# Attention's work list with empty places and one more place per step, dispatch weights of two experts in one operation, six weight blocks fetched earlier

## The chip, the cores and the metric

One core of a Trainium2 chip runs the whole program. The metric is the device time of one execution in microseconds (us); the median of three executions of the kernel before is 598.34 us.

## The reference

Three layers follow each other. B = 4 batches, H = 8 heads, S = 576 rows, 64 columns per head, 32 memory slots.

```python
a = softmax(phi, over S);  k_m = a^T k;  v_m = a^T v           # per batch and head
attn = softmax(q k_m^T / 8);  x = attn v_m                      # [4*576, 512]
p = domain_probs / sum                                          # 4 experts, dense
x = sum_e p[:, e] * (relu(x @ w1[e]) @ w2[e])                   # 512 -> 1024 -> 512
logits = x @ phi2;  d = softmax(logits, over all 2304 rows)
slot = d^T x;  slot_out[e] = relu(slot[e] @ v1[e]) @ v2[e]      # 8 experts, 4 slots each
out = softmax(logits, over 32 slots) @ slot_out                 # [2304, 512], f32
```

Here v1 and v2 are the 8 experts' weights of the third layer (moe2_w1, moe2_w2).

## The kernel before

**Units and steps.** The second layer runs in five units: units 0, 1 and 2 are batches 0, 1 and 2 with 576 rows, units 3 and 4 are the halves (288 rows) of batch 3. A unit has 8 steps, one for each half of an expert's 1024 columns. Units 3 and 4 do steps 0 and 1 together; then unit 3 does its steps 2 to 7, and then unit 4 (`MIX` is 2). A step consists of 8 places (4 for a unit of 288 rows alone). A place `at` begins with one `up`: six matmuls (lines 434 to 436) of the weights `G` with the attention result `A`, in high and low parts; ScalarE takes the result out of PSUM (line 444), and after every second `up` VectorE transposes it into `h` (line 446).

**What is put between the `up`s.** Place `at_g` (place 2 of a step with 8) issues `g_mult` for the next step: 16 matmuls (line 391) of the values `vb` with a block `raw` of w1, which SyncE fetched two steps before. Its two halves come out of PSUM in `g_out` at places 3 and 4, ScalarE (line 401) and VectorE (line 402). At place 0 the matmuls for the logits of the step before are issued (line 461). In the other places `pump` takes one entry from the list `fg` and one from the list `bg`, unless the `fg` entry is one of the heavy ones, which stand alone. An entry may be `None`: an empty place.

**The two lists.** `fg` holds the rest of the unit before: the logits' statistics, the weights `we` (line 601), five heavy blocks of `sums` (line 625, matmuls of `we` with `h`, accumulated into `srun` by VectorE, line 633 or 635), and the row softmax. `bg` holds the attention of the next batch, `attention(b)`: loads of phi, k and v; the softmax over S with the column maximum in two halves (line 159, `mx`), its turn through TensorE (lines 168, 172), the sums in two halves (line 207, `sm`) and a small matmul that gathers them (lines 243, 247); then five tiles of q, each with a turn (299), scores (315), exponential (330), normalisation (335 to 338) and a turn into `A` (346, 351, 352). Each engine runs its own instructions in the order in which the program issues them.

**Buffers.** PSUM has 4 rotating banks `at` for everything but `up` and the logits. SBUF has 2 buffers `raw`, 2 buffers `g` and 5 buffers `big`; k and v of the next batch take a `big` one, which comes free only when the `sums` of the unit before have read `h`. SyncE issues every DMA, in program order; where one waits for its buffer, all later ones wait behind it.

**The last stretch.** The third layer reads its weights in 160 blocks `v` of 256 KB each: 32 blocks of w2 (line 690), 64 of v1 (line 693) and 64 of v2 (lines 700 and 707). `fill` takes a buffer that has come free and fetches the next blocks of the list into it; `done` refills it once its blocks are used. Five blocks go early into buffers of attention, nine and then 36 into `big`, four into `A1`; after the `sums` of unit 4 come eight into `raw`, eight into `g` and four into `A0`. At the start of unit 4's step 2 the program stands thus:

```python
if us == (NU - 1,) and n == MIX:
    for _ in range(4):
        fill(bigp, "big", 9)
```

Blocks are used in the order in which they are fetched (lines 1000, 1026 and 1166).

**Unit 0** does more: in its steps 0 to 7 it also prepares `M` = w2 times phi2 (lines 488 to 514), in its step 0 it ends its own attention, and `shares` (four matmuls, line 821, and 20 copies, lines 826 and 830) spreads the shares `p`, which the `fg` entries of the unit read.

Of the kernel before, what the change touches and what calls it, by code (L numbers as in the profile page):

```python
# [8 lines left out]
F32 = mybir.dt.float32  # L9
F32R = mybir.dt.float32r  # L10
ACTF = mybir.ActivationFunctionType
ALU = mybir.AluOpType
# [4 lines left out]
def kernel(  # L17
# [23 lines left out]
    nc = tc.nc  # L41
# [3 lines left out]
    NSLOT = phi2.shape[1]  # L45
    FH = 512
    NCH = E * F // FH
# [34 lines left out]
    A = [const.tile([128, 2, 2, S], F32R, tag=f"A{n}", name=f"A{n}") for n in range(2)]  # L82
    kbd = [const.tile([128, 4, 2, NM], F32, name=f"kbd{n}") for n in range(2)]
    vb = [const.tile([128, 128], F32, name=f"vb{n}") for n in range(2)]
    M = const.tile([128, 4 * NCH, NSLOT], F32)
    srun = const.tile([128, 8, 4, 32], F32)
    mrun = const.tile([128, 1], F32)
    zrun = const.tile([128, 1], F32)
# [5 lines left out]
    def load_phi(b):  # L94

        t = att.tile([128, 36, NM], F32, tag="ph", name="ph")
        src = phi[b].rearrange("(i c) s m -> c i s m", c=2)
        for c in range(2):
            nc.sync.dma_start(
                out=t[:, 16 * c:16 * c + 16, :].rearrange("p (i r) m -> p i (r m)", i=4),  # L100
                in_=src[c, :, 0:512, :].rearrange("i (p r) m -> p i (r m)", r=4),
            )
        for c in range(2):
            nc.sync.dma_start(
                out=t[64 * c:64 * c + 64, 32:36, :],
                in_=src[c, :, 512:576, :].rearrange("i p m -> p i m"),
            )
        ph_t[b] = t
# [18 lines left out]
    def load_q(b, ti):  # L127

        t = att.tile([128, H, HD], F32, tag="q", bufs=2, name="q")
        if ti < 4:  # L130
            nc.sync.dma_start(
                out=t, in_=q[b, :, 0:512, :].rearrange("h (p r) d -> r p h d", r=4)[ti]
            )
        else:
            nc.sync.dma_start(out=t[0:64], in_=q[b, :, 512:576, :].rearrange("h s d -> s h d"))
        q_t[b, ti] = [t[:, 2 * j:2 * j + 2].rearrange("p c d -> p (c d)") for j in range(4)]
# [386 lines left out]
    def group(u):  # L523
# [10 lines left out]
        def share(e):  # L534
            return pe[:, b, tb0:tb0 + nt, e:e + 1].to_broadcast([128, nt, 32])
# [57 lines left out]
        def weights(h):  # L593

            def f():
                if h == 0:
                    st["dt"] = pc.tile([128, nt, 32], F32, tag="lt", name="dt")
                    nc.vector.transpose(out=flat(st["dt"]), in_=flat(st["lc"]))
                we = st["we", h] = pc.tile([128, nt, 2, 32], F32, tag="we", bufs=2, name="we")
                for e in range(2):  # L600
                    nc.vector.tensor_tensor(
                        out=we[:, :, e], in0=st["dt"], in1=share(2 * h + e), op=ALU.mult
                    )
                if h == 1:
                    nc.vector.tensor_copy(out=mrun, in_=st["mg"])
                    if st["first"]:
                        nc.vector.tensor_copy(out=zrun, in_=st["zg"])
                    else:
                        nc.vector.scalar_tensor_tensor(
                            out=zrun, in0=zrun, scalar=st["fo"], in1=st["zg"],  # L610
                            op0=ALU.mult, op1=ALU.add,
                        )
            return f
# [125 lines left out]
    with tc.manual_schedule():  # L739
# [94 lines left out]

        fg, bg, heavy = [], [], []

        def pump():


            f = fg.pop(0) if fg else None  # L840
            if f:
                f()
            if f in heavy:
                return
            f = bg.pop(0) if bg else None
            if f:
                f()

        def attention(b):

            kvs = kv_stages(b)
            qs = [q_stages(b, ti) for ti in range(5)]

            def load(*a):
                def f():
                    for g in a:
                        g()
                return f

            def with_q(f, m):  # L860
                def g():
                    f()
                    if m < 5:
                        load_q(b, m)
                return g
            items = [lambda: (load_phi(b), load_kv(b, 0)), lambda: load_kv(b, 1), kvs[0], kvs[1]]
            items += [kvs[2], None, kvs[3], lambda: load_q(b, 0), kvs[4]]
            items += [lambda: (load_q(b, 1), kvs[6]()), kvs[5], kvs[8], kvs[7], kvs[9], kvs[11], kvs[10]]
            items += [with_q(qs[0][0], 2), kvs[12], None, kvs[13]]
            for t in range(5):  # L870
                items.append(qs[t][1])
                items.append(with_q(qs[t + 1][0], t + 3) if t < 4 else None)
                items.append(qs[t][2])
                items.append(lambda t=t: (qs[t][3](), qs[t - 1][4]() if t else None))
            items += [None, qs[4][4]]
            return items
# [8 lines left out]
        def finish(lu, n):  # L885

            _, g_, sums, rows = groups[lu]
            if lu < NU - 2:
                rw = [None] * 5 + [f for row in rows for f in (row, None, None)]
            else:  # L890
                rw = [f for row in rows for f in (row, None)]
            if lu < NU - 2:
                ps_ = [sums(k, 5) for k in range(5)] if lu < NU - 3 else [sums(k, 4) for k in range(4)]
                fg.extend([None] * 3 + g_[:2] + [None] + g_[2:5] + [None] * 2 + ps_ + rw)
            else:
                ps_ = [sums(k, 2) for k in range(2)]
                fg.extend([None] + g_[:5] + ps_ + [None] * 4 + rw)
            heavy[:] = [g_[0]] + ps_
            if lu < NU - 3:
                bg.extend([None] * 8 + attention(lu + 2))  # L900

        for n, us in steps:
            b = units[us[0]][0]
            s = b * NCH + n
            ups = [
                (u, fb, ki) for fb in range(4) for u in us for ki in range(len(units[u][1]))
            ]
            if us == (0,) and n == 0:
                ups.sort(key=lambda x: x[2])

            if len(ups) == 8:
                at_l, at_g, at_c = 0, 2, (3, 4)
            elif n == MIX:
                at_l, at_g, at_c = 1, 2, (3,)
            else:
                at_l, at_g, at_c = int(us != (NU - 1,) or n > MIX), 0, (1, 2)
            if us == (0,) and n == 0:
                bg += attention(1)
                bg.insert(8, shares)
            if n == 0 and us[0]:  # L920
                assert len(bg) == 0
            if n % 2 == 0:
                for u in us:
                    hid_tile(u, n // 2)
            if us == (NU - 2,) and n == MIX:
                fill(att, "ph", 2, again=False)
                fill(att, "kt", 1, again=False)
                for _ in range(2):
                    fill(att, "q", 1, again=False, bufs=2)
            if us == (NU - 2,) and n == NCH - 1:  # L930
                fill(bigp, "big", 9)
            if us == (NU - 1,) and n == MIX:
                for _ in range(4):
                    fill(bigp, "big", 9)
            gs = []
            for at, (u, fb, ki) in enumerate(ups):
                up(u, n, fb, ki)
                if at in at_c and gs:
                    gs.pop(0)()
                if at == at_l:  # L940
                    for lu, ln in last:
                        logits(lu, ln)
                        if ln % 2:
                            groups[lu][0](ln // 2)
                        if ln == NCH - 1:
                            finish(lu, n)
                if at == at_g and s + 1 < NG and us != (NU - 1,):
                    gs = g_mult(s + 1)
                else:
                    pump()  # L950
                if us == (0,):
                    for f in early[at] if n == 0 else ():
                        f()
                    if n and at in (1, 2, 3, 4, 6, 7):
                        ms[n][(1, 2, 3, 4, 6, 7).index(at) + 1]()
                    if at == 5 and n + 1 < NCH:
                        ms[n + 1][0]()
            for f in gs:
                f()
            last = [(u, n) for u in us]  # L960
        (lu, ln), = last
        logits(lu, ln)
        groups[lu][0](ln // 2)
        fill(const, "A1", 4, again=False)

        g_ = groups[lu][1]
        warm2(8)
# [5 lines left out]
        warm2(6)  # L973
        for _ in range(2):
            fill(rawp, "raw", 4)
        for _ in range(2):
            fill(gp, "g", 4)
        fill(const, "A0", 4, again=False)
        rest = groups[lu][3]

# [240 lines left out]
```

## Time and profile before

| What | Value |
|---|---|
| Median of three executions | 598.34 us (596.36 to 599.28) |
| The profiled execution: time, span | 600.98 us, 599.1 us |
| TensorE matmul busy | 551.8 us, 92% |
| VectorE, ScalarE busy | 313.4 us (52%), 204.2 us (34%) |
| Mean granted TensorE clock | 0.981 of full speed |
| HBM read, written | 100.50 MB, 4.72 MB |

The span is the time from the first to the last instruction; 1.9 us of the profiled execution lie around it. TensorE's share is the union of its matmuls, of which up to a few overlap, so 92% does not say that the array works at its peak; what can be gained is read from what TensorE waits for, stretch by stretch. Unit 1 runs from about 165 to 277 us of the span, unit 2 from 277 to 388, and the last stretch, from the end of unit 4's sums, from 504 on. In the rows, "PE" is TensorE, "PEld" its weight loads, "DVE" VectorE, "ACT" ScalarE, "SPq" the issuing of DMAs by SyncE, and L159 is line 159 of the kernel.

### The profile page before, as it was taken

Reading aid. Unit: us, or ns where it says so; the run is one execution under the profiler, and the core shown is the slowest. Engines: PE = TensorE matmul, PEld = TensorE weight load, DVE = VectorE, ACT = ScalarE, POOL = GpSimd, SP = SyncE. Lnnn points to the kernel's source line nnn. Section 1 sums busy time; section 2 is a strip of 40 time slices with the busy share of each in tenths; the row PEclk is TensorE's granted clock in tenths of the full one; section 3 lists DMA queues with packets and bytes.
Section 4 is the critical chain, followed back from the end, with each engine's and each line's share of the span. In section 5 each row is a group of like instructions: output and inputs, shape, how many; then the busy total and the mean of one; then the engine's idle time right before and its main releaser. Section 6 shows DMA issues by size and latency. Waiting matters only on the chain.

```text
span 599.1 us, 15721 instructions
## 1 busy us (share of the span) xinstructions
PE 551.8 (92%) x6810; PEld 390.6 (65%) x6810; DVE 313.4 (52%) x693; ACT 204.2 (34%) x509; POOL 28.3 (5%) x34
## 2 busy tenths in 40 slices
PE   8887999999999899999989999999989998999993
PEld 7675778777776668877657787766557685324342
DVE  5656646864581566677345677761567362012022
ACT  2332445444451244554123344530444130102022
POOL 0000000101000001100000101000010000000000
PEclk9989999999999889999998899999999999999998
DMA  8992455444141733332446232440550398999998
GB/s 216 317 317 72 159 160 167 142 141 142 71 148 46 234 94 102 102 124 71 121 132 197 81 105 72 130 170 4 174 196 0 120 369 300 361 355 388 360 352 279
DMA packets 92771, 106.22 MB, mean 177 GB/s; under 512 B 30752, under 2 KB 55840, under 8 KB 92704
## 3 DMA queue, kind: packets, MB, share of 16 engines
q1 hardware_dynamic: 92704, 105.24, 54.2%
q8 instruction: 53, 0.87, 0.6%
q14 instruction: 14, 0.11, 0.1%
HBM read 100.50 MB, written 4.72 MB: 176 GB/s over the span
## 4 chain that ended last, share of the span: by engine, by line
PE 65%; DVE 14%; DMA 11%; issue 4%; ACT 3%; SPq 1%; POOL 0%; ACTq 0%; DVEq 0%; POOLq 0%
PE mm L434 11%; DMA v<-in_moe_w_dram 11%; PE at L625 9%; PE mm L436 9%; PE mm L435 9%; PE lb L461 6%; PE at L391 5%; DVE g L402 3%; PE at L315 3%; DVE h L446 2%; PE at L488 2%; PE mm L767 2%; PE at L299 1%; PE at L223 1%; ACT hT L444 1%
## 5 line engine op out<-in xcount | busy, mean ns | idle before, releaser
L444 ACT ACTIVATE hT<-mm 128x288 f32<-128x288 f32 x256 | 105.1, 411 | 235.0 <-PE mm L436 204.2
L446 DVE STREAM_TRANSPOSE h<-hT 128x576 f32<-128x576 f32 (+1 forms) x160 | 104.0, 652 | 138.6 <-ACT hT L444 126.8
L434 PE MATMUL mm<-A,g 128*128 128x288 f32 x512 | 170.4, 333 | 2.1 <-ACT g L401 1.0
L436 PE MATMUL mm<-A,g 128*128 128x288 f32 x512 | 153.2, 299 | 2.6 <-DVE g L402 2.6
L435 PE MATMUL mm<-A,g 128*128 128x288 f32 x512 | 152.6, 298 | 0.8 <-DVE A L352 0.8
L434 PEld LDWEIGHTS mm<-A,g 128*128 128x128 f32 x512 | 98.0, 191 | 48.9 <-ACT hT L444 20.4
L436 PEld LDWEIGHTS mm<-A,g 128*128 128x128 f32 x512 | 97.8, 191 | 3.9 <-DVE g L402 3.9
L435 PEld LDWEIGHTS mm<-A,g 128*128 128x128 f32 x512 | 98.3, 192 | 1.3 <-DVE A L352 1.0
L625 PE MATMUL at<-h,we 32*32 32x256 f32 x2304 | 58.3, 385 | 6.3 <-issue 4.4
L625 PEld LDWEIGHTS at<-h,we 32*32 32x32 f32 x2304 | 34.7, 103 | 25.5 <-issue 10.7
L402 DVE TENSOR_TENSOR g<-at,g 128x512 fp32r<-128x512 f32 x64 | 42.5, 671 | 5.5 <-ACT g L401 5.3
L461 PE MATMUL lb<-hT,M 128*32 128x288 f32 x512 | 40.8, 425 | 1.6 <-DVE M L514 1.6
L401 ACT CAST g<-at 128x512 fp32r<-128x512 f32 x64 | 37.2, 583 | 0.0
L391 PE MATMUL at<-raw,vb 64*32 64x512 f32 x512 | 36.5, 601 | 0.3 <-DVE srun L635 0.2
L1166 PE MATMUL mm<-v,hz 128*8 128x256 f32 x256 | 34.4, 380 | 0.6 <-DVE mm L1053 0.6
L1166 PEld LDWEIGHTS mm<-v,hz 128*8 128x8 f32 x256 | 13.3, 88 | 19.9 <-DMA v<-in_moe_w_dram 5.2
L488 PE MATMUL at<-ident,w 128*128 128x128 f32 x128 | 20.5, 284 | 3.3 <-issue 1.3
L461 PEld LDWEIGHTS lb<-hT,M 128*32 128x32 f32 x512 | 13.1, 111 | 15.0 <-issue 5.8
L541 DVE STREAM_TRANSPOSE lt<-lb 128x288 f32<-128x288 f32 x32 | 14.6, 470 | 14.6 <-PE lb L461 13.7
L1026 PE MATMUL mm<-v,sT 128*32 128x512 f32 x128 | 21.2, 597 | 0.9 <-DMA v<-in_moe_w_dram 0.5
L488 PEld LDWEIGHTS at<-ident,w 128*128 128x128 f32 x128 | 14.6, 143 | 10.6 <-issue 3.1
L552 POOL TENSOR_TENSOR lt<-lt,pe 128x576 f32<-128x576 f32 (+1 forms) x10 | 9.9, 989 | 226.3 <-DVE lt L541 226.3
(153 smaller groups left out, 523.7 us busy)
## 6 DMA issues: line engine op xcount, KB each, us to landing
v<-in_moe_w_dram SPq DMA_DIRECT2D x160, 256.0 KB, 5.7
raw<-in_moe_w_dram SPq DMA_DIRECT2D x32, 1024.0 KB, 5.1
w<-in_moe_w_dram SPq DMA_DIRECT2D x16, 512.0 KB, 6.9
kv<-in_k_dram SPq DMA_DIRECT2D x8, 512.0 KB, 4.8
kv<-in_v_dram SPq DMA_DIRECT2D x8, 512.0 KB, 6.1
out_dram<-ot SPq DMA_DIRECT2D x16, 256.0 KB, 4.1
q<-in_q_dram SPq DMA_DIRECT2D x12, 256.0 KB, 5.3
ph<-in_phi_dram SPq DMA_DIRECT2D x8, 256.0 KB, 5.6
```

Source lines behind the costliest of these rows:

```text
L391: nc.tensor.matmul(ts[c][32 * i:32 * i + 32, :], vb[b % 2][64 * c:64 * c + 64, 32 * i:32 * i + 32], raw[s][64 * c:64 * c + 64, i, :], star ...
L401: nc.scalar.copy(out=hi, in_=t)
L402: nc.vector.tensor_tensor(out=lo, in0=t, in1=hi.bitcast(F32), op=ALU.subtract)
L434: nc.tensor.matmul(ps, gh, ah, start=(c == 0), stop=False)
L435: nc.tensor.matmul(ps, gh, al, start=False, stop=False)
L436: nc.tensor.matmul(ps, gl, ah, start=False, stop=(c == 1))
L444: nc.scalar.activation(out=t[:, o0 - base:o1 - base], in_=ps, func=ACTF.Relu)
L446: nc.vector.transpose(out=hid[u, n // 2][:, :, 4 * (n % 2) + fb], in_=t[:, 0:o1 - base])
L461: nc.tensor.matmul(lb[u, ki][32 * a:32 * a + 32, 0:o1 - o0], M[:, 4 * n + a, :], hT[u, n, a][:, o0 - base:o1 - base], start=(f == 0), stop ...
L488: nc.tensor.transpose(t[:, 128 * c:128 * c + 128], st["w"][:, a, 128 * c:128 * c + 128], ident)
L625: nc.tensor.matmul(ts[p][32 * e:32 * e + 32, 0:256], st["we", e // 2][rows, tb, e % 2], hid[u, e][rows, tb].rearrange("p k f -> p (k f)"), ...
L1166: nc.tensor.matmul(accs[acc][32 * i:32 * i + 8, 0:256], hz[:, dh != 2, f, i, :], blk[:, 256 * m:256 * m + 256], start=(dh == 2 and f == 0) ...
```

## The change

There are five edits.

1. `pump` gets a flag. At the place of `g_mult` it now runs for `bg` alone, so that `bg` has 8 places per step and `fg` still 7.
2. Attention's list has empty places again (`lead` of them after the loads, and single ones), its loads stand three entries earlier, and a few entries change order: the sums' second half directly before the second heavy matmul block, the turn of k before the first half of v.
3. In unit 0 both halves of `g_out` run at place 3, and `shares` stands at place 3 of step 0, in one of the empty places.
4. `weights` makes `we` of two experts in one multiplication with four-dimensional operands, in place of two.
5. `fill(gp, "g", 4)` stands at the start of unit 4's step 2, in front of the four fills of `big`, in place of one of the two after the sums; `M`'s buffer, free after the last logits, takes two blocks after `A1`'s.

```diff
+    M = const.tile([128, 4 * NCH, NSLOT], F32, tag="M", name="M")
...
-                for e in range(2):
-                    nc.vector.tensor_tensor(
-                        out=we[:, :, e], in0=st["dt"], in1=share(2 * h + e), op=ALU.mult
-                    )
+                nc.vector.tensor_tensor(
+                    out=we, in0=st["dt"].unsqueeze(2).to_broadcast([128, nt, 2, 32]),
+                    in1=pe[:, b, tb0:tb0 + nt, 2 * h:2 * h + 2].unsqueeze(3).to_broadcast(
+                        [128, nt, 2, 32]
+                    ), op=ALU.mult,
+                )
...
-        def pump():
+        def pump(both=True):
...
-            f = fg.pop(0) if fg else None
+            f = fg.pop(0) if fg and both else None
...
-            items = [lambda: (load_phi(b), load_kv(b, 0)), lambda: load_kv(b, 1), kvs[0], kvs[1]]
-            items += [kvs[2], None, kvs[3], lambda: load_q(b, 0), kvs[4]]
-            items += [lambda: (load_q(b, 1), kvs[6]()), kvs[5], kvs[8], kvs[7], kvs[9], kvs[11], kvs[10]]
-            items += [with_q(qs[0][0], 2), kvs[12], None, kvs[13]]
+            items = [lambda: (load_phi(b), load_kv(b, 0)), lambda: load_kv(b, 1)] + [None] * lead
+            items += [kvs[0], kvs[1], kvs[2], None, None, kvs[3], lambda: load_q(b, 0), kvs[4], kvs[5]]
+            items += [lambda: (load_q(b, 1), kvs[6]()), kvs[7], kvs[8], kvs[9], None, kvs[10]]
+            items += [kvs[11], with_q(qs[0][0], 2), kvs[12], None, kvs[13]]
...
-                bg.extend([None] * 8 + attention(lu + 2))
+                bg.extend([None] * 5 + attention(lu + 2, 5))
...
-                bg += attention(1)
-                bg.insert(8, shares)
+                bg += attention(1, 4)
+                bg[3] = shares
...
             if us == (NU - 1,) and n == MIX:
+                fill(gp, "g", 4)
                 for _ in range(4):
...
                     gs.pop(0)()
+                    if us == (0,):
+                        gs.pop(0)()
...
-                else:
-                    pump()
+                pump(not gs or at != at_g)
...
         fill(const, "A1", 4, again=False)
+        fill(const, "M", 2, again=False)
...
-        for _ in range(2):
-            fill(gp, "g", 4)
+        fill(gp, "g", 4)
```

## Rows read from the trace of the kernel before

**Rows 1.** The page: busy share of the DMA engines in 40 slices of 15 us.

```profile
DMA  8992455444141733332446232440550398999998
```

**Rows 2.** The chain that ended last, stretch from 490 us (start, length, what).

```profile
507.89 6.60 DMA v<-in_moe_w_dram
...
574.15 4.02 DMA v<-in_moe_w_dram
```

**Rows 3.** Windows of the last stretch: busy time, then clock, DMA share, GB/s.

```profile
490.00:500.00 10.00, 9.44 (x245) 7.41 (x243) 3.93 (x12) 1.21 (x4) 0.00 (x0) 1.00 1.05 382
500.00:510.00 10.00, 7.58 (x127) 4.41 (x131) 2.58 (x7) 0.59 (x1) 0.52 (x1) 1.00 0.75 247
```

**Rows 4.** Waits of SyncE's queue: us in total, times, longest.

```profile
SPq L122 <- PE at L625: 35.5, 2, 18.4
SPq L690 <- PE at L625: 34.6, 1, 34.6
...
SPq L693 <- PE at L625: 3.7, 1, 3.7
```

**Rows 5.** Waits from 507 to 586 us.

```profile
PEld mm L1026 <- DMA v<-in_moe_w_dram: 9.5, 19, 1.4
```

**Rows 6.** TensorE's timeline at the end of unit 4's step 2.

```profile
456.22 0.29 PE L436 MATMUL mm<-A,g 128*128 128x288 f32 x1
```

**Rows 7.** Waits of TensorE in unit 1 (165 to 277 us).

```profile
PE at L172 <- DVE mx L159: 2.3, 2, 1.2
PE at L346 <- DVE ex L338: 1.0, 1, 1.0
PE at L243 <- DVE sm L207: 0.9, 1, 0.9
```

**Rows 8.** Windows in unit 1: busy time, then clock, DMA share, GB/s.

```profile
200.60:204.00 3.40, 1.66 (x12) 1.21 (x10) 3.29 (x5) 1.67 (x5) 0.00 (x0) 1.00 1.02 280
204.00:207.40 3.40, 2.83 (x12) 2.83 (x13) 1.94 (x4) 0.41 (x1) 0.00 (x0) 0.50 1.06 362
...
221.07:224.48 3.41, 3.41 (x24) 2.29 (x28) 1.07 (x5) 0.41 (x1) 0.00 (x0) 0.50 0.02 5
```

**Rows 9.** The chain from 196 to 222 us, unit 1 (start, length, what).

```profile
195.99 0.70 PE at L625 x31
...
202.07 0.93 DVE mx L159
...
203.59 0.94 DVE mx L159
...
205.04 0.24 PE mm L434
...
208.09 0.14 PE mm L434
...
211.78 1.02 PE at L391 x16
...
219.70 0.93 DVE sm L207
```

**Rows 10.** VectorE's timeline there; in brackets its idle time before.

```profile
200.71 0.78 DVE L446 STREAM_TRANSPOSE h<-hT 128x576 f32<-128x576 f32 x1 [1.95 <-ACT hT L444]
```

**Rows 11.** SyncE's timeline in unit 1.

```profile
196.51 1.74 SPq L122 DMA_DIRECT2D kv<-in_k_dram  x2
...
200.86 1.35 SPq L370 DMA_DIRECT2D raw<-in_moe_w_dram  x1
```

**Rows 12.** That block of `raw` alone: us from issue to landing.

```profile
DMA to landing us min/median/max: 9.1/9.1/9.1
```

**Rows 13.** TensorE's timeline in unit 0, steps 0 and 1.

```profile
47.54 0.33 PE L172 MATMUL at<-ident,mx 128*128 128x128 f32 x1 [1.80 <-DVE mx L159]
...
57.43 0.63 PE L488 MATMUL at<-ident,w 128*128 128x128 f32 x4 [1.35 <-issue]
```

**Rows 14.** Instructions that read or write `pe`: ns min, median, max; starts; forms.

```profile
L601 DVE TENSOR_TENSOR we<-dt,pe x20: 417/718/759, 173.2 to 495.4; 128x576 f32<-128x576 f32 x12, 128x288 f32<-128x288 f32 x8
L826 DVE COPY pe<-at x16: 135/158/159, 56.9 to 58.3; 128x16 f32<-128x16 f32 x16
...
L830 DVE COPY pe<-at x4: 149/150/150, 57.2 to 58.4; 128x8 f32<-128x8 f32 x4
```

More of the change, by code (lines that the diff above doesn't have):

```diff
@@ L84 @@
     vb = [const.tile([128, 128], F32, name=f"vb{n}") for n in range(2)]
-    M = const.tile([128, 4 * NCH, NSLOT], F32)
+    M = const.tile([128, 4 * NCH, NSLOT], F32, tag="M", name="M")
     srun = const.tile([128, 8, 4, 32], F32)
@@ L847, in pump, with attention @@
                 f()
-        def attention(b):
+        def attention(b, lead):
             kvs = kv_stages(b)
```

## The prediction

> **What bounds the kernel now.** I read the page first, then the chain that ended last, then each stretch's waits. The page's DMA row splits the run: after the first three slices mostly 1 to 5 tenths, 0 in slice 30 (from 450 us), then 8 or 9 in every slice from 480 us on [rows 1]. The chain agrees: from 507.89 us it runs from one transfer of `v` to the next, to 578 us [rows 2]. So the last stretch ends when the last `v` block has come; TensorE waits there for blocks with time to spare, 9.5 us in the v1 phase alone [rows 5]. Before that TensorE is the bound, and what can be won is its idle time. In unit 1 three waits make 4.2 us of it, all on VectorE, for `mx`, for `ex` and for `sm` [rows 7]; the same three, equally long, stand in unit 2. Behind two of them the granted clock is 0.50 for 3.4 us, that is 1.2 of 2.4 GHz, and matmuls come every 0.24 us instead of 0.14 [rows 8, 9].
>
> **Edit 5, the six blocks.** SyncE's order decides. The second fill of `big` waits 34.6 us for the `sums` of unit 3 [rows 4], and meanwhile nothing moves [rows 1]. The four `g` blocks are now in front of it. Their buffer is that of unit 4's step 2, whose last matmul is at 456.22 us [rows 6]; they are issued just behind that and land in the idle time before 472 us. The only thing queued behind them on SyncE is the fill of `big` that waits anyway. At 382 GB/s a block of 262,144 bytes takes 0.69 us [rows 3], so four taken out of the full stretch are worth 2.7 us. Nothing excludes less, if the stream stops later for a buffer: bound 0.
>
> The two `M` blocks go into a hole. SyncE has no buffer left and waits 3.7 us for unit 4's `sums` [rows 4]; the rate falls from 382 to 247 GB/s over 10 us, which is 1.35 MB or 3.5 us lost [rows 3]. Two more blocks fill 1.4 us of it for certain. If the queue does not run empty, its slow restart goes too, and all 3.5 us come back. I take 2.2 us, nearer to the sure part, because the two blocks alone cover less than half of the wait. One of the two later `g` fills remains; its buffer (unit 4's `h`) is released by the same `sums`. Should it get the buffer of the four early blocks instead, it would wait for the w2 phase to read them, some 3 us after the last `raw` issue, with eight transfers under way to cover it: at most 1 us. Edit 5: -4.9 us, between 0 and -6.2.
>
> Beside the row stands a page: the Trainium skill, "DMA: Bandwidth & Descriptors", section Specifications, gives about 358 GB/s from HBM to one core. The trace's 382 GB/s over 10 us is above it [rows 3]. By the page a block would take 0.73 us and edit 5 would give some 0.2 us more.
>
> **Edits 1 and 2 in units 1 and 2.** I wrote down for both kernels which entry falls on which place. Three things move.
>
> `mx`: before, its halves are issued at places 3 and 4 of step 2 and the turn at place 5, and VectorE does `g_out` and `mx` in turn, 0.93 us each time for `mx` [rows 9], while TensorE stands 2.3 us. After, the first half is issued at place 2, where VectorE is idle for 1.95 us [rows 10], the second at 3, the turn at 4. VectorE saves one `mx` and one `g_out` of the queue, TensorE arrives one `up` (0.8 us) earlier. That leaves 2.3 + 0.8 - 0.93 less part of a 0.65 us `g_out`, some 1.8 us: -0.5.
>
> `sm`: the second half moves from place 6 to place 4, the matmul that needs it from 7 to 6. VectorE has done it when TensorE comes: of 0.9 us [rows 7] I leave 0.1: -0.8.
>
> `ex`: the last normalisation now has `g_mult` (1.02 us [rows 9]) between it and its turn. Of 1.0 us [rows 7] I leave 0.1: -0.9.
>
> Half speed: about 14 matmuls at 0.24 instead of 0.14 us [rows 9] make some 1.4 us for each of the two spells in a unit. The one behind `sm` should go with its wait, the one behind `mx` may stay, as 1.8 us of standing remain. I take one of two: -1.4.
>
> What it costs: k and v are now asked for in step 0, and SyncE waits there for the `big` buffer until the `sums` end, as before [rows 4]. Now the `raw` block of step 1 is queued behind it. Before, the block issued in that spot (for a step later) went at 200.86 us and landed 9.1 us later [rows 11, 12], 13.3 us after the `sums` end at 196.7; `g_mult` comes 15.1 us after it [rows 9], and with the savings above about 12.9. So a wait of 0.4 us, 0.2 on average over the two clock cases. And five more entries per unit now stand behind `g_mult`, which holds two of the four banks: no row shows the price; between nothing (VectorE and ScalarE are idle there, [rows 10]) and one `g_out` (0.65 us) each, 3.3 us. I take 0.8.
>
> Per unit -0.5 - 0.8 - 0.9 - 1.4 + 0.2 + 0.8 = -2.6, for both -5.2. Bounds: 0 (each stall only moves) and, with all waits and half-speed spells gone, 2 x (4.2 + 2.8) = -14.
>
> **Edits 1 to 3 in unit 0.** The wait for `mx` (1.80 us) and the one behind `shares` (1.35 us) [rows 13] go, since `mx` gets two places more and `shares` leaves step 1. In step 0 `shares` puts 20 copies of 0.15 us [rows 14], overlapped some 1.6 us, ahead of VectorE's share of unit 0's last q tiles, for which the next `up` waits: +1.2 to +1.6, less what that wait hides. -3.15 + 1.6 = -1.5; bounds 0 and -3.1.
>
> **Edit 4.** 288 more elements cost 0.30 us (718 against 417 ns) [rows 14], so 1152 cost 0.72 + 0.60 = 1.32 against 1.44 us: 0.1 us for each of ten. Only in unit 4, where nothing else runs, are two of them on the path: -0.2. Above, if the four-dimensional form cost as much more as 288 further elements, 0.3 us each: +0.6.
>
> The Trainium skill, "VectorE: DVE Perf Modes", section on the TRN2 errata, says that a VectorE operation between SBUF tensors pays a fixed 58 cycles (60 ns) each. By that the ten would save 0.6 us in all, by the rows 1.2; on the path 0.1 against 0.2.
>
> **The sum.** -4.9 - 5.2 - 1.5 - 0.2 = -11.8 us. The profiled execution took 600.98 us, so 589.2; it lies 2.6 us over the median of 598.34, which becomes 586.5. A change under 0.5% (3 us) cannot be told from none here.
>
> **The rivals.**
> - *Only the last stretch gains* (0.20). VectorE has the same work in a unit; a wait taken from `mx` or `sm` may come back at an entry behind `g_mult`. For it: VectorE is 3.29 of 3.40 us busy around the `mx` wait [rows 8]. Against: right before that it is idle 1.95 us [rows 10]. 598.3 - 4.9 - 0.2 = 593.2.
> - *Only the front gains* (0.08): the stream is held up again by a buffer, so that 160 blocks end no earlier. Against: TensorE's 9.5 us of waiting [rows 5]. 598.3 - 6.9 = 591.4.
> - *More than forecast* (0.07): no half-speed spell is left and the hole in the stream closes wholly: 2.8 + 1.3 + 1.6 us more, 580.8.
> - *Nothing to be measured* (0.08): half of the last stretch, the rest given back: 596.
> - *Slower* (0.07): the `raw` block that now waits behind k and v. Every us by which it comes after `g_mult` stands in full, once in unit 1 and once in unit 2. To eat 11.8 us and 3 more it has to be 7.4 us late each time, 20 us after the `sums` end instead of 13.3. For it: 9.1 us to land [rows 12] while k and v are moving at 362 GB/s [rows 8]. Against: it is now the first block behind them, as the later one was. From 7.4 us on it decides; at 8 us the time is 602.5.
>
> **The numbers.** My forecast has 0.50: 586.5, own range 581 to 591. The range of 8 in 10 takes in the gain in the last stretch alone and the larger gain: 578 to 594. Faster by over 0.5%: 0.50 + 0.20 + 0.08 + 0.07 = 0.85; within: 0.08; slower: 0.07.
>
> **What would show it.** In the changed kernel's trace: four `v` blocks issued near 450 us and the DMA share no longer falling between 502 and 507 us; the last `v` earlier by 5 us relative to unit 4's `sums`; in units 1 and 2 the `sm` and `ex` waits gone, `mx` still there at under 2 us, two clock falls instead of four; `shares` at some 39 us; ten `we` operations of 1.3 and 0.7 us. It is wrong if TensorE's idle time in units 1 and 2 stays at 4 us each, if `g_mult` waits for a DMA in step 3, or if the `v` stream shows a new gap.

## The result and the profile after

The changed kernel takes 580.88 us (median of four executions, 580.06 to 581.87), the kernel before 598.81 us (four, 596.36 to 601.11): ratio 0.9702, interval 0.966 to 0.9744. The forecast was 586.5 us with a range of 578 to 594. The profiled execution took 581.87 us, its span is 579.9 us, that is 19.1 us less than before.

Where the 19.1 us are is read from two points in each trace. Unit 4's `sums` end at 490.2 us instead of 504.0: 13.8 us come from the units ahead of it. From there to the end of the span it is 89.7 us instead of 95.1: 5.3 us come from the last stretch. Of the 13.8 us, 12.1 are in units 1 and 2, which run from 159.8 to 379.4 us in before and take 207.5 us after instead of 219.6; a unit is counted here from ScalarE's last copy of an `up` (L444) of one unit to that of the next. Behind unit 2, up to the `sums` of unit 4, it is 122.5 us instead of 124.5, and unit 0 ends 0.3 us later than before. 1.5 of the 2.0 us behind unit 2 are in the first four places of the step that units 3 and 4 do together: in before the last turn for batch 3 stands there, with its wait for `ex`, which no longer comes after.

```profile
380.01 0.30 PE L346 MATMUL at<-ident,ex 64*128 64x64 f32 x2 [1.02 <-DVE ex L338]
```

The page of the kernel after, its span, two of its rows of 40 slices, and the shares of the chain; then the shares of the chain before:

```profile
span 579.9 us, 15699 instructions
...
PEclk9979999999999999999999999999999999999997
DMA  8993655424440493326029332440552299999998
...
PE 79%; DVE 10%; DMA 4%; ACT 3%; issue 3%; POOL 0%; DVEq 0%; ACTq 0%; POOLq 0%; SPq 0%
```

```profile
PE 65%; DVE 14%; DMA 11%; issue 4%; ACT 3%; SPq 1%; POOL 0%; ACTq 0%; DVEq 0%; POOLq 0%
```

The stream of `v` now keeps the DMA engines at 9 tenths for seven slices on end, where there was an 8 among them before [rows 1]. The chain has 4% of its length on DMA instead of 11%, so by the chain TensorE bounds more than half of the last stretch too. The clock row is below 9 only near the two ends of the run.

The waits of TensorE in units 1 and 2 of the kernel after, from 160 to 268 and from 270 to 368 us, answer to [rows 7]:

```profile
PE at L172 <- DVE mx L159: 1.8, 1, 1.8
PE at L243 <- DVE sm L207: 0.4, 1, 0.4
...
PE at L391 <- DVE srun L637: 0.2, 1, 0.2
```

The first two rows stand in both units, the third in unit 2 alone. Of 4.2 us of standing per unit 2.2 are left, and the wait for `ex` is gone. The windows of the kernel after at the places of [rows 8] and [rows 3] (busy time of TensorE, its weight loads, VectorE, ScalarE and GpSimd, then granted clock, DMA share, GB/s):

```profile
490.00:500.00 10.00, 9.60 (x88) 4.25 (x84) 2.58 (x7) 0.58 (x1) 0.53 (x1) 1.00 0.89 280
500.00:510.00 10.00, 8.78 (x79) 3.35 (x76) 1.11 (x3) 1.46 (x3) 0.00 (x0) 1.00 1.05 388
204.00:207.40 3.40, 3.40 (x35) 2.54 (x34) 2.51 (x5) 1.28 (x4) 0.00 (x0) 1.00 1.06 387
217.00:220.00 3.00, 3.00 (x31) 2.13 (x31) 1.96 (x7) 1.28 (x3) 0.00 (x0) 1.00 0.04 9
```

Behind both turns (that of `mx` at 202.5 us, that of `sm` at 216.4) the clock is 1.00, that is 2.4 GHz, where it was 0.50; none of the four falls of units 1 and 2 is left, in this profile or in that of any kernel below that has the further place in these units. The hole in the stream behind the `sums` is still there: 280 GB/s in the ten us behind their end, at 490.2 us. SyncE's waits show the early blocks of `g`:

```profile
SPq L692 <- PE mm L436: 17.6, 1, 17.6
...
SPq L692 <- PE at L627: 14.2, 1, 14.2
```

The long wait for the `sums` of unit 3 [rows 4] is cut in two: SyncE first waits for the last `up` of unit 4's step 2, issues the four blocks at 442.8 us, and then waits 14.2 us for the `sums`.

### The profile page after: what moved, and what is told of

The parts are those of the page before. It is cut to its first block, busy times and chain, and to the rows that moved or that the text cites. A ratio compares the mean times of both kernels' runs of the same rounds, so it can differ in the third digit from the quotient of the medians.

```text
span 579.9 us, 15699 instructions
## 1 busy us (share of the span) xinstructions
PE 541.9 (93%) x6810; PEld 388.3 (67%) x6810; DVE 314.1 (54%) x683; ACT 204.2 (35%) x509; POOL 28.3 (5%) x34
## 4 chain that ended last, share of the span: by engine, by line
PE 79%; DVE 10%; DMA 4%; ACT 3%; issue 3%; POOL 0%; DVEq 0%; ACTq 0%; POOLq 0%; SPq 0%
PE mm L434 13%; PE mm L436 10%; PE mm L435 10%; PE at L627 9%; PE lb L461 6%; PE at L391 5%; DMA v<-in_moe_w_dram 4%; PE at L315 3%; PE mm L1030 3%; PE at L488 3%; DVE h L446 2%; PE mm L1170 2%; DVE g L402 2%; PE mm L769 2%; PE at L500 1%
## 5 line engine op out<-in xcount | busy, mean ns | idle before, releaser
L444 ACT ACTIVATE hT<-mm 128x288 f32<-128x288 f32 x256 | 105.6, 413 | 227.8 <-PE mm L436 197.7
L434 PEld LDWEIGHTS mm<-A,g 128*128 128x128 f32 x512 | 96.9, 189 | 48.6 <-issue 26.8
L436 PEld LDWEIGHTS mm<-A,g 128*128 128x128 f32 x512 | 96.8, 189 | 3.9 <-DVE g L402 3.9
L435 PEld LDWEIGHTS mm<-A,g 128*128 128x128 f32 x512 | 97.2, 190 | 1.3 <-DVE A L352 1.0
L627 PE MATMUL at<-h,we 32*32 32x256 f32 x2304 | 55.4, 385 | 5.1 <-issue 2.6
L627 PEld LDWEIGHTS at<-h,we 32*32 32x32 f32 x2304 | 33.4, 103 | 22.7 <-issue 7.5
L461 PE MATMUL lb<-hT,M 128*32 128x288 f32 x512 | 39.5, 413 | 0.7 <-DVE M L514 0.7
L315 PEld LDWEIGHTS at<-kbd,qt 128*128 128x128 f32 (+1 forms) x160 | 18.2, 184 | 8.8 <-DVE A L352 3.3
L461 PEld LDWEIGHTS lb<-hT,M 128*32 128x32 f32 x512 | 12.9, 109 | 13.4 <-issue 5.3
L315 PE MATMUL at<-kbd,qt 128*128 128x64 f32 (+1 forms) x160 | 20.0, 270 | 1.6 <-DVE A L352 1.4
```

What stands on the lines that cost most here:

```text
L315: nc.tensor.matmul(sc[0:n, :, j, :], st["qt"][:, j, 0:n], kbd[b % 2][:, j], start=True, stop=True)
L434: nc.tensor.matmul(ps, gh, ah, start=(c == 0), stop=False)
L435: nc.tensor.matmul(ps, gh, al, start=False, stop=False)
L436: nc.tensor.matmul(ps, gl, ah, start=False, stop=(c == 1))
L444: nc.scalar.activation(out=t[:, o0 - base:o1 - base], in_=ps, func=ACTF.Relu)
L461: nc.tensor.matmul(lb[u, ki][32 * a:32 * a + 32, 0:o1 - o0], M[:, 4 * n + a, :], hT[u, n, a][:, o0 - base:o1 - base], start=(f == 0), stop ...
```

## The experiments

Each is compared with the kernel before on the same chip; the medians of before were 599.05, 599.9 and 599.59 us in the three sets (`e1_fills`, `e5_g`, `e6_m` and `e2_front`; then `e3_clock`, `e4_loads`, `e8_mx` and `e7_unit0`; then the other four). "After" is the changed kernel.

### Edit 5, and its two halves

`e1_fills` is before with edit 5 alone, `e5_g` with its first half, `e6_m` with its second.

```diff
 e1_fills, e5_g:
+                fill(gp, "g", 4)
                 for _ in range(4):
                     fill(bigp, "big", 9)
...
-        for _ in range(2):
-            fill(gp, "g", 4)
+        fill(gp, "g", 4)
 e1_fills, e6_m:
+        fill(const, "M", 2, again=False)
```

> The kernel before with edit 5 alone: four v blocks into a g buffer at the start of unit 4's step 2, two into M's buffer. My theory: the last stretch is bound by the stream of v blocks and gains what the profiles of before and after show for it (span 599.1 to 579.9, unit 4's sums earlier by 13.8, so 5.4 us for the stretch): 4.5 to 6 us faster. Rival: the stretch gained because everything in front of it came earlier and the stream was less disturbed; then edit 5 alone gives under 2 us.

> The kernel before with the four early g blocks alone, no M blocks. My theory: four blocks at 0.69 us leave the full stretch, 2.7 us faster; the hole in the stream at the wait for unit 4's sums stays (rate near 250 GB/s there). Rival, the hole is what decides: under 1 us, since the same wait still empties the queue.

> The kernel before with the two M blocks alone. My theory: between 1.4 us (two blocks' worth) and 3.5 us (the queue no longer runs empty, the whole hole closes), forecast 2.2. Rival: the M fill is issued at the same full rate as the rest and only shifts the hole by 1.4 us, 0 to 1 us faster.

| Kernel | us | Ratio (interval) | End of `sums` to end of span, us |
|---|---|---|---|
| before | 599.05 | | 95.1 |
| `e1_fills` | 595.44 | 0.9924 (0.9887 to 0.996) | 90.4 |
| `e5_g` | 595.61 | 0.9947 (0.9922 to 0.9971) | 91.8 |
| `e6_m` | 598.6 | 0.9986 (0.9962 to 1.0011) | 93.9 |

The last column is from the one profiled execution of each. By it edit 5 is worth 4.7 us, the blocks of `g` 3.3 and those of `M` 1.2; by the ratios 4.6, 3.2 and 0.8 us of 599, the last not to be told from nothing. The two halves add up to the whole within the intervals. What the two `M` blocks do to the hole is seen in three windows around the end of the `sums`, which end at 504.0 us in before and at 503.6 in `e6_m`. Before:

```profile
494.00:504.00 10.00, 7.45 (x293) 4.93 (x291) 2.07 (x8) 0.00 (x0) 0.00 (x0) 1.00 0.91 337
504.00:514.00 10.00, 9.57 (x84) 4.15 (x84) 2.56 (x7) 0.59 (x1) 0.52 (x1) 1.00 0.87 278
514.00:524.00 10.00, 8.78 (x80) 3.50 (x76) 1.11 (x3) 1.65 (x3) 0.00 (x0) 1.00 1.04 376
```

And `e6_m`:

```profile
494.00:504.00 10.00, 7.93 (x290) 5.23 (x288) 1.54 (x7) 0.00 (x0) 0.00 (x0) 0.90 1.04 378
504.00:514.00 10.00, 9.76 (x84) 4.66 (x83) 2.15 (x7) 0.58 (x1) 0.52 (x1) 0.93 0.96 315
514.00:524.00 10.00, 8.78 (x79) 3.41 (x76) 1.11 (x3) 1.52 (x3) 0.00 (x0) 1.00 0.97 330
```

In the first two windows 41 and 37 GB/s more are 0.78 MB, three blocks; in the third 46 GB/s less take 0.46 MB of it back. What is left is 0.32 MB, 1.2 blocks, 0.8 us at 382 GB/s [rows 3]. The hole is filled early and opens again later.

Shorter windows show that it has two parts. In before the queue does run dry, and then the rate stays low although the DMA engines are busy:

```profile
503.50:504.50 1.00, 1.00 (x17) 0.60 (x6) 0.51 (x2) 0.00 (x0) 0.00 (x0) 1.00 0.19 43
506.00:513.00 7.00, 6.76 (x64) 2.40 (x66) 0.69 (x1) 0.59 (x1) 0.52 (x1) 1.00 0.95 308
```

And in `e6_m`:

```profile
503.50:504.50 1.00, 1.00 (x8) 0.94 (x5) 0.92 (x3) 0.00 (x0) 0.00 (x0) 0.50 0.77 262
509.00:511.00 2.00, 2.00 (x24) 0.56 (x20) 0.00 (x0) 0.00 (x0) 0.00 (x0) 1.00 0.80 198
```

The DMA share at the end of the `sums` is 0.77 instead of 0.19: with the two blocks the queue no longer runs dry. The low rate behind it comes all the same, 198 GB/s at a share of 0.80 from 509 to 511 us, where the full stream moves 378 at 1.04. So the packets themselves take longer there, and this is no restart of an empty queue; what makes them longer, no run here shows.

### The front alone

`e2_front` is after without edit 5 (the diff above, undone).

> The changed kernel without edit 5: both g fills again after the sums, no M blocks. My theory: the two parts of the gain add, so it is 5 us slower than the changed kernel and 13 us faster than before (585 to 587). Rival: the stretch in front gains only because the fills moved, or the parts overlap: within 2 us of the changed kernel.

Measured: 585.29 us, 0.978 (0.9752 to 0.9809). So edits 1 to 4 are worth some 13 us of 599, about twice the 6.9 us forecast for them. To 0.9702 of the whole, 0.8% are missing: edit 5 gives as much behind them as alone. Within the intervals the two gains add up, as the sum assumed. In the profile unit 0 ends at 158.3 us, before at 159.8, each with one clock fall of 3.4 us in it; units 1 and 2 are 12.1 us shorter.

### The clock by itself

`e3_clock` is before with idle matmuls of the identity, written to columns that nobody reads, in front of the turns that wait for `mx` (four each) and `sm` (three), in units 1 and 2. Nothing else is changed, so the waits on VectorE stand where they stood.

```diff
+                if b > 1:
+                    for _ in range(4):
+                        nc.tensor.matmul(t1[:, 384:512], ident, ident, start=True, stop=True)
...
+                if c and b > 1:
+                    for _ in range(3):
+                        nc.tensor.matmul(t3[:, 384:512], ident, ident, start=True, stop=True)
```

> The kernel before with dummy matmuls in the waits of units 1 and 2 alone: four before each of the two turns of mx (about 1.0 us each, no longer than the wait), three before the second gather of sm (0.75 us). They add nothing to the result and nothing to the path. My theory: the clock falls of units 1 and 2 come from TensorE standing there and are worth about 1.4 us each beside the waits, so the four falls vanish while the waits stay: 4 to 6 us faster. Rival: the falls come from what is issued there (small matmuls, transposes) or cost nothing on the path: falls still there, or time within 1.5 us of before.

Measured: 592.17 us, 0.9871 (0.9842 to 0.99). The windows of [rows 8] in this kernel:

```profile
204.00:207.40 3.40, 3.40 (x34) 2.54 (x34) 2.42 (x5) 0.98 (x3) 0.00 (x0) 1.00 1.05 333
221.07:224.48 3.41, 3.41 (x35) 2.40 (x35) 1.24 (x3) 0.85 (x3) 2.29 (x2) 1.00 0.00 0
```

All four falls are gone (1.00 for 0.50, 35 matmuls in the second window for 24), and steps 2 to 4 of units 1 and 2 together are 5.85 us shorter, 1.46 us for each fall. The rest of the 7.7 us of the ratio is in step 1, which is 1.9 us shorter; why is taken up below. So behind each of the waits, of 2.3 us for `mx` (in two pieces) and of 0.9 us for `sm`, some 1.5 us more were lost at half the clock. Filling the waits with useless work won this second loss back, and not the waits themselves.

### Where the loads stand

`e4_loads` is after, with the entries of phi, k and v at places 3 and 4 of step 1, as in before, where they stand behind that step's `g_mult`.

```diff
-                bg.extend([None] * 5 + attention(lu + 2, 5))
+                bg.extend([None] * 10 + attention(lu + 2, 0))
```

> The changed kernel with attention's two load entries moved back to where they stood in step 1 (places 3 and 4 of before); every other entry stays at its place. My theory: the phi and k loads of before fell into the sums of step 1 and held up TensorE's instructions there (waits named issue: 3.50 us for a block of sums in unit 1 and 4.5 us in unit 2, 2.76 after the change); so the second block of sums takes 3.5 us again and it is 1 to 3 us slower than the changed kernel (582 to 584). Rival: the place of the loads gives nothing, step 1 is as short as in the changed kernel, time 580 to 581.5.

Measured: 585.43 us, 0.9752 (0.9718 to 0.9786), 0.5% more than after; the intervals overlap. The profile is clearer: step 1 of units 1 and 2 takes 16.1 and 17.7 us instead of 15.1 and 15.4, 3.3 us together, and all other steps are equal within 0.05 us. SyncE's timeline in unit 1, after first:

```profile
165.44 0.37 SPq L370 DMA_DIRECT2D raw<-in_moe_w_dram  x1
165.91 1.01 SPq L99 DMA_DIRECT2D ph<-in_phi_dram  x2
...
195.94 0.93 SPq L122 DMA_DIRECT2D kv<-in_k_dram  x2
...
200.48 1.70 SPq L370 DMA_DIRECT2D raw<-in_moe_w_dram  x2
```

Then `e4_loads`:

```profile
164.52 10.22 SPq L370 DMA_DIRECT2D raw<-in_moe_w_dram  x2
174.83 1.01 SPq L99 DMA_DIRECT2D ph<-in_phi_dram  x2
```

Phi is issued 9 us later, right behind a `raw` that waits for its buffer: what sets when its DMA goes is not the place of its entry alone but the `raw` in front of it on SyncE. And while phi and the first blocks of k arrive during the `sums`, TensorE waits there for "issue", that is for nothing that the profile names, 0.4 us in unit 1 and 1.7 us in unit 2:

```profile
PE at L627 <- issue: 1.7, 1, 1.7
```

After has no such wait in these units. The two named waits are 2.1 of the 3.3 us; the rest is not named.

### The list, the place, and the order in it

`e10_list` is after with the list of before in units 1 and 2 (no empty places, old order, eight empty entries ahead), with the further place kept. `e8_mx` issues both halves of `mx` at place 2 of step 2. `e11_raw` is `e8_mx` with the entries of k and v moved behind the `g_mult` of step 1, so that the `raw` goes in front of them again.

```diff
 e10_list:
-                bg.extend([None] * 5 + attention(lu + 2, 5))
+                bg.extend([None] * 8 + attention(lu + 2, 0))
 e8_mx, e11_raw:
-            items += [kvs[0], kvs[1], kvs[2], None, None, kvs[3], lambda: load_q(b, 0), kvs[4], kvs[5]]
+            items += [lambda: (kvs[0](), kvs[1]()), None] if lead == 5 else [kvs[0], kvs[1]]
+            items += [kvs[2], None, None, kvs[3], lambda: load_q(b, 0), kvs[4], kvs[5]]
 e11_raw:
+            if lead == 5:
+                items = [lambda: load_phi(b)] + [None] * 4
+                items += [lambda: load_kv(b, 0), lambda: load_kv(b, 1)]
...
```

> The changed kernel with the list of before in units 1 and 2 (eight empty places in front, loads, then the rest without the empty ones), but with the further place per step: the entries run earlier. My theory: the empty places matter, since mx then comes two places after phi is asked for, VectorE stands until phi has landed (5 to 6 us) and g_out and the sums wait behind it: 4 to 10 us slower than the changed kernel (585 to 591). Rival: the further place alone brings the gain and the empty places nothing: within 2 us of it.

> The changed kernel with both halves of mx at place 2 of step 2 in units 1 and 2, where VectorE is idle, an empty place at 3 and the turn still at 4. My theory: the remaining wait of 1.8 us for mx, twice, is the second half queued behind the transpose and g_out; it falls under 0.3 us and the kernel becomes 2.5 to 3.6 us faster than the changed one (577 to 578.5). Rival: VectorE's total work in that step is the bound and the wait moves to g_out or the next turn: within 1 us of the changed kernel.

> As the run with both halves of mx at place 2 of step 2, and in units 1 and 2 the entries that load k and v at places 3 and 4 of step 1 again, behind the raw block of that step; phi is still loaded in step 0. My theory: g_mult of step 3 waited 1.3 and 1.6 us for the raw block queued behind k and v, which gave back most of what mx had gained; that wait goes, step 3 is short again, 2.5 to 3 us faster than that run (576 to 577), and sums stay at 2.76 us since phi no longer loads during them. Rival: the loads of k and v themselves, not phi, held up the sums of before, then step 1 is longer by 1 to 2 us and nothing is won.

| Kernel | us | Ratio (interval) | Units 1 and 2, us | Steps 1 | Steps 2 | Steps 3 |
|---|---|---|---|---|---|---|
| before | | | 219.6 | 33.3 | 42.6 | 23.7 |
| after | 580.88 | 0.9702 (0.966 to 0.9744) | 207.5 | 30.5 | 39.3 | 25.5 |
| `e10_list` | 579.36 | 0.9684 (0.9649 to 0.9719) | 207.0 | 32.4 | 37.8 | 25.8 |
| `e8_mx` | 579.08 | 0.9675 (0.9637 to 0.9713) | 206.8 | 30.5 | 35.3 | 28.7 |
| `e11_raw` | 578.45 | 0.9657 (0.9621 to 0.9693) | 204.1 | 30.9 | 35.3 | 25.7 |

The last four columns are from the profiled execution; a step goes from one step's last ScalarE copy of an `up` to the next one's, and the steps of units 1 and 2 are added.

`e10_list` fell out against my theory. I had expected 585 to 591 us, since the empty places and the new order were to bring most of the gain; in units 1 and 2 the further place brings all of it without them. Its waits in unit 1:

```profile
PE at L346 <- DVE ex L338: 1.0, 1, 1.0
PE at L627 <- DVE g L402: 0.9, 1, 0.9
PE at L223 <- ACT ph L203: 0.3, 1, 0.3
PE at L391 <- DVE srun L635: 0.2, 1, 0.2
```

The waits for `mx` and `sm` and all four clock falls are gone without any empty place; the one for `ex` stays, and one of 0.9 us behind `g_out` comes into the `sums`. The loads move with the place too: phi goes out at 161.48 us, in step 0, since with eight places to a step its entry is reached before the `g_mult` of step 1. The list of after ends the wait for `ex` and has a shorter step 1, but keeps 1.8 us of waiting for `mx`. One against the other, nothing is left.

`e8_mx` takes that wait away: steps 2 are 4.0 us shorter. Steps 3 give 3.3 of it back, and TensorE's timeline in unit 1 of `e8_mx` shows to what:

```profile
206.37 0.66 PE L391 MATMUL at<-raw,vb 64*32 64x512 f32 x8 [1.33 <-DMA raw<-in_moe_w_dram]
```

In its unit 2 the waits have the same:

```profile
PE at L391 <- DMA raw<-in_moe_w_dram: 1.6, 1, 1.6
```

This is the rival that was to make the kernel slower: the `raw` behind k and v, which in after lands at 208.4 us, 0.75 us in front of its `g_mult`. As soon as the step is 2 us shorter, it is late. `e11_raw` puts it in front of the loads, and the waits of unit 1 are then:

```profile
PE at L243 <- DVE sm L207: 0.4, 1, 0.4
PE at L391 <- DVE srun L635: 0.2, 1, 0.2
```

Units 1 and 2 are 3.5 us shorter than in after. By the ratios the whole is 2.7 us shorter, with intervals that overlap, and the 576 to 577 us that I had expected were not reached. This profile shows 10.2 us at half the clock in unit 0, as that of after does, where that of `e8_mx` shows 6.8; its executions spread from 576.7 to 580.4. The loads of k stand in step 1 again here and those of phi do not; step 1 is 0.4 us longer than in after, where `e4_loads`, with both moved, has 3.3. So it is above all phi whose loading during the `sums` goes with the loss there.

### Unit 0, and the best version

`e7_unit0` is after without the further place in unit 0 (`shares` thereby comes at place 4 of step 0). `e12_best` has this and `e11_raw` together.

```diff
-                pump(not gs or at != at_g)
+                if us != (0,) or not gs or at != at_g:
+                    pump(not gs or at != at_g)
```

> The changed kernel without the further place in unit 0 (pump isn't called at the place of g_mult there; units 1 and 2 keep it). My theory: in unit 0 the further place costs, since scores and turns there stand behind g_mult in want of a bank (waits of 1.06 and 0.38 us at L315, 1.3 us at L488): 1.5 us faster than the changed kernel, step 4 short again (about 16.6 us). Rival: the entries only move and as much is waited for elsewhere: within 0.7 us.

> The same and, in unit 0, no further place behind g_mult. My theory: the gains add, 2 to 3.5 us more, 573 to 575. Rival: unit 0's gain in the earlier run was a clock fall that happened not to come; then the same time as the run without it.

Measured: `e7_unit0` 578.55 us, 0.9644 (0.9616 to 0.9672), whose interval still overlaps with that of after; `e12_best` 573.45 us, 0.9572 (0.9539 to 0.9606). The waits in unit 0 (36 to 160 us), after:

```profile
PE at L823 <- DVE g L402: 1.5, 2, 1.3
PE at L315 <- DVE A L352: 1.4, 2, 1.1
PE at L488 <- DVE g L402: 1.3, 4, 0.5
PE lb L461 <- DVE M L514: 0.7, 1, 0.7
PE mm L434 <- ACT A L351: 0.4, 1, 0.4
```

And `e7_unit0` (36 to 155 us):

```profile
PE lb L461 <- DVE M L514: 2.2, 3, 1.1
PE at L488 <- DVE g L402: 1.5, 2, 1.0
PE mm L434 <- ACT A L351: 0.4, 1, 0.4
PE at L315 <- DVE g L402: 0.3, 1, 0.3
PE at L346 <- DVE ex L338: 0.2, 1, 0.2
```

The place that helps units 1 and 2 costs time in unit 0, which has the work on `M` in the same places: without it steps 1 to 7 take 106 instead of 107.3 us. Step 0 ends at 47.2 us in `e7_unit0` and 47.3 in `e12_best`, without a clock fall, and in the kernels with the place between 48.4 us (`e10_list`, no fall there) and 53.0 us (`e9_we`, 10.2 us at half the clock). Without a fall on either side the place thus costs 2.6 us: unit 0 ends at 153.1 us in `e7_unit0` and at 155.7 in `e10_list`. The other 4.4 us to the 160.1 of after are the clock, and so the rival of `e12_best` is right in part: its time came as expected, but it is 5.0 us below `e11_raw` instead of 2 to 3.5. The wait of 1.3 us for `shares` (L823), behind which the clock falls in after, is gone; but `e10_list` has the same wait of 1.3 us and no fall, so the wait alone does not decide, and whether the falls stay away for want of the place is not shown. `e12_best` is 1.3% faster than the changed kernel.

### The weights

`e9_we` is after with the two multiplications of before for `we`.

> The changed kernel with two multiplications per we again. My theory: 0.1 us for each of ten operations, only those of unit 4 on the path: 0.2 us slower at most, not to be told from the changed kernel in the time; VectorE's rows show 2 x 0.72 in place of 1.34 us. Rival: the one long operation delays the transposes and g_out behind it, then it is faster than the changed kernel.

Measured: 582.55 us, 0.973 (0.9692 to 0.9767): not to be told from after. The operations in unit 1, after first, then before:

```profile
L600 DVE TENSOR_TENSOR we<-dt,pe 128x1152 f32<-128x1152 f32 x2 | 2.7, 1337 | 0.0
```

```profile
L601 DVE TENSOR_TENSOR we<-dt,pe 128x576 f32<-128x576 f32 x4 | 2.8, 744 | 0.0
```

One of 1337 ns stands for two of 744: 0.15 us saved each time, where the rows of the forecast gave 0.12 and its other sum 0.06. The form with four dimensions costs nothing more. The 58 cycles of that other sum, from the Trainium skill, "VectorE: DVE Perf Modes", section on the TRN2 errata, are a row of a table that the same section corrects below it, to a measured fixed term of about 150 cycles. At the 0.96 GHz of the same table that is an estimate of 156 ns, and the 151 ns here agree with it.

## Why the prediction was right, and where not

The direction and the range of 8 in 10 were right. The time was 5.6 us below the forecast and just below the forecast's own range of 581 to 591; what was missing is in units 1 and 2 and the turn right behind them.

| Step | Forecast, us | Measured, us | From |
|---|---|---|---|
| Edit 5: `g` blocks | -2.7 | -3.3 | `e5_g` |
| Edit 5: `M` blocks | -2.2 | -1.2 | `e6_m` |
| Units 1, 2: waits for `mx`, `sm`, `ex` | -4.4 | -4.0 | after |
| Units 1, 2: clock | -2.8 | -5.85 | `e3_clock` |
| Units 1, 2: `raw`, and what waits behind `g_mult` | +2.0 | 0 | after |
| Units 1, 2: step 1 | none | -2.8 | after, `e4_loads` |
| Unit 0 | -1.5 | -1.5 | `e2_front` |
| Weights | -0.2 | not to be told from 0 | `e9_we` |

- **Edit 5** came as forecast in its sum, from the right order of SyncE's queue; the last `v` lands 74.8 us behind the end of the `sums` instead of 80.4. The reason for the hole was wrong: "If the queue does not run empty, its slow restart goes too" has its condition met in `e6_m` (a share of 0.77 instead of 0.19), and the low rate came all the same. Only the sure part came, 1.2 us for 1.4. The 388 GB/s of the full stream after are again above the some 358 GB/s of the Trainium skill, "DMA: Bandwidth & Descriptors", section Specifications; the measurement decides.
- **The waits.** `mx` fell by 0.5 us per unit as worked out (1.8 left), `ex` by 1.0 for 0.9. `sm` kept 0.4 us where I left 0.1. The second wait for `ex` stands behind the last `up` of unit 2 and so outside the 12.1 us.
- **The clock** is the step that failed most: "the one behind `mx` may stay, as 1.8 us of standing remain. I take one of two." Its price was right, 1.46 against 1.4 us for each; its number was not, all four went. In after TensorE stands 1.8 us in one piece and keeps 2.4 GHz; before, it fell to 1.2 GHz behind two waits for `mx` of 1.2 us at most each, and behind one of 0.9 us for `sm`. The length of the standing did not tell which, and which other thing does is not shown.
- **The costs** "I take 0.8" and the 0.2 us for `raw` did not come. No wait stands behind `g_mult` in units 1 and 2 of after, and `raw` arrives in time; `e8_mx` shows how narrowly. The forecast had `raw` 13.3 us behind the end of the `sums` and `g_mult` at 12.9, though the savings it names give 15.1 - 0.5 - 1.4 = 13.2; in unit 1 of after they came at 12.2 and 13.0.
- **Not priced** was what moves with the loads. I counted their place as a cost only, and left out the 1.4 us for "issue" that stand in the `sums` of units 1 and 2 beside the three waits. That phi no longer arrives during the `sums` takes such waits out of step 1: 2.8 us against before, 3.3 against `e4_loads`.
- **Unit 0** came to the -1.5 us where the time at half the clock was equal (`e2_front`), and by its terms: step 0 is 0.1 us shorter (forecast -1.8 + 1.6), steps 1 to 7 are 1.5 us shorter (-1.35). In the profiled execution of after it is lost again to 6.8 us more at half the clock, and `e7_unit0` shows that without the further place more was to be had.
- **What edit brought it.** The prediction went through the new list entry by entry. `e10_list` shows that the further place of edit 1 does it and that the empty places and the new order add nothing to it that can be measured. The new list without the place was not run.
- **A number met by luck.** The rival *More than forecast* (0.07) named 580.8 us, the measured time to 0.1 us. Only one of its two conditions came, that no half-speed spell is left in units 1 and 2. The hole did not close, the last 1.6 us of its sum have no reason beside them, and step 1, which filled their place, is not in it.

The rows added up, without the weights: -3.3 - 1.2 - 4.0 - 5.85 - 2.8 - 1.5 = -18.7 us, against -17.9 in the medians. The rows come from several kernels, with one profile each. The two profiled executions differ by 19.1 us without the 1.5 us of unit 0, so some 2.2 us of theirs stand in no row: 0.8 in the last stretch, 0.4 in units 1 and 2 and 1.0 behind them.

Left open: why TensorE waits for "issue" in the `sums`. In units 1 and 2 of before and of the kernels with edit 5 or half of it alone it is 1.4 us, equal in each, and in those with phi loaded early it is gone. But `e3_clock` has phi and k where before has them, with no such wait in these units, and its step 1 in unit 2 takes 15.5 us instead of 17.3. So it goes with the sequence of instructions as well as with what is being loaded, and no run here tells these apart.

## What to carry to other kernels

Where a wait of TensorE is followed by a stretch at half the granted clock, count both: here the second was as dear as the first, and it went as soon as the waits were spread or filled. Try a further place for a list before reordering it, since here it did by itself what the reordering was meant to do, and check it in each unit, since the same place cost time in the unit that had other work there. When a load is moved, look at what stands in front of it and behind it on the issuing queue; the transfer that is late next shows only when the compute ahead of it gets shorter.

## What the runs showed of the hardware

- A few matmuls whose result nobody reads, put into waits of 0.9 and 2.3 us, kept the granted clock at 1.00 and made the kernel 1.3% faster (`e3_clock`); 5.85 us of the 7.7 lie in the steps with the falls.
- The clock falls of units 1 and 2 came at the same times in before and `e1_fills` (204, 221, 317 and 334 us), while `e6_m`, with the same front, has three, at 205, 222 and 331 us. Those of unit 0 differ between kernels with the same unit 0: 10.2 us at half the clock in after, 3.4 in `e2_front`, none in `e10_list`. Unit 0 ends 4.4 us later in after than in `e10_list`, so this alone may move an execution by that much.
- A stream at 376 to 389 GB/s fell behind the `sums` to 278 GB/s over 10 us in before and 280 in after. A queue that has run dry is only part of it: in `e6_m`, where it did not, the rate was 198 GB/s from 509 to 511 us with the DMA engines busy at a share of 0.80.
